# Threshold attention and a hard-swish feed-forward layer in one kernel: scores issued slot by slot at the start, projections from slot 11, products two slots sooner

## The chip, the cores and the metric

The kernel runs on one core of a Trainium2 chip. The metric is the device time of one execution in microseconds (us); lower is better. Three runs of the kernel before took 533.33, 536.99 and 535.21 us, a median of 535.21.

## The reference

Eight batches, eight heads, 576 positions, 64 dimensions per head. Attention keeps only keys whose score lies within `tau` of the row's maximum; its output goes through a feed-forward layer with 2,048 hidden units.

```python
scores = scale * np.matmul(q, k.transpose(0, 1, 3, 2))
thresh = np.max(scores, axis=-1, keepdims=True) - tau
scores = np.where(scores >= thresh, scores, -1000000000.0)
scores = scores - np.max(scores, axis=-1, keepdims=True)
attn = np.exp(scores)
attn = attn / (np.sum(attn, axis=-1, keepdims=True) + 1e-09)
x = np.matmul(attn, v)          # then (B * S, H * D)
h = x @ w_in
g = h * np.clip(h + 3.0, 0.0, 6.0) / 6.0
out = g @ w_out
```

## The kernel before

**Slots.** The work is cut into 144 slots, 18 to a batch (`NSLOT`). A slot is 128 query rows of two heads (a head pair's two halves lie in one slot; 576 keys each), or, in the two slots that hold the last 64 rows of each head, 64 rows of four heads. A Python loop (L467) walks over the slots and writes out every instruction in the order in which each engine takes it; nothing is reordered later. Each engine works through its own list in order, and waits where an operand isn't there yet.

**What a slot's attention takes.** TensorE (PE) computes the scores in fp32 (`burst`, L208) into the eight banks of the accumulator memory `ps`. VectorE (DVE) passes over each head's scores once (`sm_max`, L238): it copies them to `s` and takes the row maximum. GpSimd (POOL) makes the bias (L247), ScalarE (ACT) masks (L252) and takes the exponential with its sum (L257), DVE the reciprocal (L260), POOL normalises to bf16 `pn` (L265). The weights `pn` are then transposed into `pT` (or `pR`, for the slots of last rows): for most slots by a DMA that SyncE's queue (SP) issues (L276), for some early slots (`sl.on_chip`, L194) by PE and a copy by DVE (`pe_transpose`, L278). `pn` has four buffers, so that the normalisation of slot n+4 waits until slot n's transpose has landed.

**Products, projections, second layer.** `av_main` and `av_rest` (L293, L300) multiply transposed weights with V into one of two banks (`bank`, L178), and DVE copies the result to `xT` or `xR`. A chunk is 256 query rows of one batch. When its fourth head pair has been multiplied (`multiply`, L401), eight items for the first layer are put on a list, `todo1`. An item (`mm1`, L315) is 32 matmuls into one bank; then ACT (in odd slots) or DVE (in even ones) adds 3 and clips at 0 (`mm1_relu`), and DVE multiplies (`mm1_gate`, L346) into `g`. One item is taken in each slot from slot `N1` = 15 on. When a chunk's items are done, eight parts of the second layer go on `todo2`; odd slots take two of them (`second`, L457). DVE copies a finished tile to `osb` (L365) and SP writes it out (L378).

**The order in a slot** (loop at L467): the two DVE passes of slot n+1; reciprocal of n-1; copies left from the slot before; the projection's matmuls; products due in this slot; the projection's elementwise part; on-chip transposes of n-2; second layer; exponentials of n; masks of n+1; `jobs` (DVE's block transposes of Q and K); normalisation of n-1 on POOL, and its transpose's issue on SP; in even slots the burst for slots n+2 and n+3; then `issues` (loads on SP and POOL).

**Bursts.** Slots n and n+1 share two of the banks. In a burst the steps for both are interleaved, and the last ones, in the shared banks, are held by a no-op on POOL that itself waits for an earlier step of the burst (L213, L228). A burst starts only after DVE has passed over both slots before.

**Due slots** (L393 to L447) are written out by hand. With n0 = 18 b: products of the first chunk at n0 + 8, 10, 12, 14, of the second at n0 + 18, 20, 22, 24, of the last rows at n0 + 16. `load` (L82) loads one quad (four heads of a batch) of K in one piece or of Q in four. Weights are loaded in four pieces each by POOL's queue, w_in in slots 4, 6, 8, 10 and w_out in slots 12, 13, 14, 15; V in eight pieces per batch. After the loop, what is left of `todo1`, `todo2` and the last batch's products is worked off (L544 to L555).

Of the kernel before, what the change touches and what calls it, by code (L numbers as in the profile page):

```python
# [20 lines left out]
def kernel(  # L21
# [18 lines left out]
    N1 = 15  # L40
# [111 lines left out]
    load(0, 1, 10, T, by=nc.scalar)  # L152
    load(0, 0, 4, T)
    load(1, 1)
# [34 lines left out]
    for b in range(B):  # L189
        for g, t in ((0, 0), (0, 1), (1, 0), (1, 1), (None, 4), (0, 2), (0, 3), (1, 2), (1, 3)):  # L190
            for i in range(2):
                sl = Slot()
                sl.b, sl.g, sl.t, sl.i, sl.n = b, g, t, i, len(queue)
                sl.on_chip = sl.n in (1, 3, 5, 7, 8, 9, 11)  # L194
                queue.append(sl)
# [12 lines left out]
    def burst(n):  # L208
        steps = ((0, 0, P, 0), (1, 0, OWN, 0), (0, 0, P, 1), None,
                 (0, P, OWN, 0), (1, 0, OWN, 1), (0, P, OWN, 1), (1, OWN, P, 0), (1, OWN, P, 1))  # L210
        for step in steps:
# [6 lines left out]
            for a in range(2):  # L218
                c = 32 * (2 * i + a)
                c0 = score_col(n + i, a) + k0  # L220
                for quad, rows, q0 in (((2 * sl.b + sl.g, slice(0, P), sl.t * P),) if sl.t < 4 else
# [5 lines left out]
                    if (i, k0) == (1, OWN):  # L227
                        behind(mm, relay)  # L228

# [63 lines left out]
    def av_main(b, hp, chunk):  # L293
        if hp == chunk == 0:
            xT[b] = x_pool.tile([P, KI, 512], BF16, tag="xT", name="xT")
        pb = bank()[:, 0:256]
# [97 lines left out]
    for b in range(B):  # L394
        n0 = b * NSLOT
        for hp in range(NPAIR):
            at(products, n0 + 8 + 2 * hp, (b, hp, 0))
            at(products, n0 + 18 + 2 * hp, (b, hp, 1))
        at(products, n0 + 16, (b, None, None))
# [15 lines left out]
    for quad in range(2, 2 * B):  # L415
        b, g = divmod(quad, 2)
        n0 = (b - 1) * NSLOT
        when = (((4, 5), (7, 8))[g] if b == 1 else ((-2, -1), (6, 7))[g])
# [6 lines left out]
    at(jobs, 0, lambda: transpose_q(0, 4, 8))  # L425
    for n, job in ((0, lambda: transpose_k(1, 0)), (1, lambda: transpose_k(1, 1)), (2, lambda: transpose_q(1, 0, 8)),
                   (3, lambda: transpose_q(0, 8, T)), (5, lambda: transpose_q(1, 8, T))):
        at(jobs, n, job)
# [13 lines left out]
    for b in range(1, B):  # L442
        v_pieces(b, (16, 17, 18, 19, 20, 21, 22, 23) if b == 1 else [(b - 1) * NSLOT + n for n in range(8, 24, 2)])
    for i, n in enumerate((4, 6, 8, 10)):
        at(issues, n, lambda i=i: load_w_in(i))
    for i, n in enumerate((12, 13, 14, 15)):
# [5 lines left out]
    burst(0)  # L452
    sm_max(queue[0])
    for i in range(2):
# [11 lines left out]
    waiting = []  # L466
    for n, sl in enumerate(queue):  # L467
        now = n
        late_slot = n == len(queue) - 2
# [6 lines left out]
        waiting = []  # L476
        item = None
# [4 lines left out]
        multiply(n)  # L482
        if item:
            mm1_gate(item, h, mm1_relu(h, on_act=n % 2 == 1))
        if n > 1 and queue[n - 2].on_chip:
# [7 lines left out]
        if part == 3:  # L493
            waiting.append(lambda tile=(bb, mt): late.extend(mm2_out(*tile, on_act=False)))
# [5 lines left out]
        if n % 2 == 0 and n + 2 < len(queue):  # L500
            burst(n + 2)
        if n < 3 or n == 6:
# [6 lines left out]
    for copy in waiting:  # L509
        copy()  # L510
# [39 lines left out]
    for n in range(len(queue), len(queue) + 7):  # L550
# [39 lines left out]
```

## Time and profile before

| | |
|---|---|
| median of three runs | 535.21 us |
| profiled execution, its own time | 535.49 us |
| span, first to last instruction | 533.7 us |
| mean granted clock of PE | 0.971 of full speed |
| PE busy | 501.8 us (94%), 6,735 matmuls |
| DVE busy | 446.7 us (84%) |
| ACT busy | 442.6 us (83%) |
| POOL busy | 281.1 us (53%) |
| score matmuls (L224) | 190.4 us |
| first layer (L313, w_in) | 133.8 us |
| second layer (L313, w_out) | 130.7 us |
| products (L290) | 46.5 us |
| chain that ended last | PE 80%, DMA 4%, DVE 2% |
| DMA moved | 80.85 MB, 151 GB/s over the span |
| w_in piece, issue to landing | 8.3 us (median of 4) |
| w_out piece, issue to landing | 10.6 us (median of 4) |
| transposes pT by DMA, issue to landing | 4.0 us (median of 123) |

Busy times are unions of an engine's instructions within the span. PE runs several matmuls of a few rows at once, and their ends are modelled, so that the sums by line overlap. The chain follows the last instruction back to what released it, step by step.

### The profile page before, as it was taken

How to read it: one execution, taken by the hardware profiler on the slowest of the kernel's cores; microseconds unless marked ns; L12 is line 12 of the kernel's file. 1: busy time of each engine (PE TensorE's matmuls, PEld its weight loads, DVE VectorE, ACT ScalarE, POOL GpSimd, SP SyncE). 2: the span in 40 equal slices, each digit the busy share in tenths (PEclk: the TensorE clock that was granted, in tenths of full speed). 3: DMA queues.
4: the chain of work that ended last, by engine and by line, in shares of the span. 5: the costliest groups of instructions: out<-in, count | busy, mean ns of one | idle time of the engine just before them, and what ended most of it. 6: DMA issues, size and time to landing. Idle time of an engine off the chain costs nothing.

```text
span 533.7 us, 17090 instructions
## 1 busy us (share of the span) xinstructions
PE 501.8 (94%) x6735; PEld 371.2 (70%) x6739; DVE 446.7 (84%) x1141; ACT 442.6 (83%) x949; POOL 281.1 (53%) x512
## 2 busy tenths in 40 slices
PE   6677787999999999999999999999999999999997
PEld 6454565677777777677767777677767777778465
DVE  6664776799999999999999999999999998887433
ACT  3776676899999999999999999999999999999322
POOL 1664564655565665566665655555555556555000
PEclk9987788899999999999999999999999999999999
DMA  8499699998999969898979999997999987856511
GB/s 176 57 160 218 106 128 178 174 215 136 156 161 180 184 138 185 142 174 155 194 144 183 175 157 174 160 186 127 169 169 197 159 111 143 143 111 113 120 60 41
DMA packets 229969, 80.85 MB, mean 151 GB/s; under 512 B 210688, under 2 KB 223232, under 8 KB 229888
## 3 DMA queue, kind: packets, MB, share of 16 engines
q1 hardware_dynamic: 216016, 70.12, 77.1%
q0 software_dynamic: 13440, 8.92, 14.1%
q8 instruction: 53, 0.87, 0.7%
q10 hardware_dynamic: 432, 0.72, 0.4%
q14 instruction: 28, 0.23, 0.1%
HBM read 36.70 MB, written 9.44 MB: 86 GB/s over the span
## 4 chain that ended last, share of the span: by engine, by line
PE 80%; DMA 4%; DVE 2%; issue 1%; ACT 0%; POOLq 0%; POOL 0%; DVEq 0%
PE ps L313 46%; PE ps L224 27%; PE ps L290 6%; DMA pT<-pn 4%; DVE s L238 1%; PE ps L518 1%; ACT r L331 0%; DVE g L346 0%; DVE xT L298 0%; DVE osb L521 0%; POOLq L265 0%; POOL pn L265 0%; DVE rinv L260 0%; DVEq L260 0%; DVEq L238 0%
## 5 line engine op out<-in xcount | busy, mean ns | idle before, releaser
L238 DVE TENSOR_SCALAR_CACHE_REDUCE s<-ps 128x576 f32<-128x576 f32 x288 | 205.6, 751 | 42.5 <-PE ps L224 23.5
L252 ACT ACTIVATE s<-s,bias 128x576 f32<-128x576 f32 x288 | 205.9, 763 | 25.6 <-POOL bias L247 25.4
L265 POOL TENSOR_SCALAR pn<-s,rinv 128x576 bf16<-128x576 f32 x288 | 210.9, 745 | 23.3 <-DMA pT<-pn 4.2
L224 PE MATMUL ps<-kT,qT 32*128 32x128 f32 (+3 forms) x2560 | 190.4, 438 | 21.7 <-DVE s L238 11.7
L257 ACT ACTIVATE s<-s 128x576 f32<-128x576 f32 x288 | 192.4, 671 | 0.0
L224 PEld LDWEIGHTS ps<-kT,qT 32*128 32x128 f32 (+1 forms) x2560 | 135.4, 182 | 63.3 <-DVE s L238 16.4
L313 PE MATMUL ps<-xT,w_in_sb 128*64 128x256 bf16 (+1 forms) x1936 | 133.8, 277 | 0.1
L313 PE MATMUL ps<-w_out_sb,g 128*64 128x512 bf16 (+1 forms) x1021 | 130.7, 379 | 0.2
L313 PEld LDWEIGHTS <-w_in_sb 128*64 128x64 bf16 (+1 forms) x1936 | 110.2, 110 | 28.6 <-issue 18.3
L247 POOL TENSOR_SCALAR bias<-m 128x2 f32<-128x2 f32 (+1 forms) x146 | 27.6, 189 | 175.9 <-DVE rinv L260 165.4
L346 DVE SCALAR_TENSOR_TENSOR g<-r,ps 128x512 bf16<-128x512 f32 x128 | 87.8, 687 | 10.7 <-ACT r L331 6.3
L313 PEld LDWEIGHTS <-g 128*64 128x64 bf16 (+1 forms) x1024 | 61.7, 109 | 47.9
L331 ACT ACTIVATE r<-ps,three 128x512 f32<-128x512 f32 x81 | 55.3, 686 | 40.7 <-PE ps L313 39.7
L257 ACT ACTIVATION_READ_ACCUMULATOR s<-s 128x1 f32 x288 | 54.8, 190 | 0.0
L290 PE MATMUL ps<-pT,v 128*64 128x256 bf16 x640 | 46.5, 277 | 0.8 <-DVE s L238 0.8
L290 PEld LDWEIGHTS <-v 128*64 128x64 bf16 x960 | 42.0, 112 | 3.6 <-issue 1.5
L333 DVE TENSOR_SCALAR r<-ps 128x512 f32<-128x512 f32 x63 | 42.9, 681 | 0.0
L126 POOL DMA_DIRECT2D v<-in_v_dram x64 | 36.7, 574 | 9.4 <-issue 3.5
L298 DVE CAST xT<-ps 128x256 bf16<-128x256 f32 x64 | 26.8, 419 | 11.3 <-PE ps L290 11.1
L365 DVE TENSOR_SCALAR osb<-ps 128x512 f32<-128x512 f32 x32 | 21.5, 672 | 9.1 <-PE ps L313 9.1
L118 DVE STREAM_TRANSPOSE kT<-nk 128x320 f32<-128x320 f32 (+1 forms) x64 | 26.5, 453 | 1.0 <-DMA nk<-in_k_dram 1.0
L104 DVE STREAM_TRANSPOSE qT<-nq 128x640 f32<-128x640 f32 (+2 forms) x33 | 24.8, 751 | 0.0
(31 smaller groups left out, 143.2 us busy)
## 6 DMA issues: line engine op xcount, KB each, us to landing
nk<-in_k_dram SPq DMA_DIRECT2D x15, 576.0 KB, 5.8
nq<-in_q_dram SPq DMA_DIRECT2D x60, 144.0 KB, 5.6
out_dram<-osb SPq DMA_DIRECT2D x31, 256.0 KB, 2.9
v<-in_v_dram POOLq DMA_DIRECT2D x32, 80.0 KB, 3.9
v<-in_v_dram POOLq DMA_DIRECT2D x32, 64.0 KB, 3.5
w_in_sb<-in_moe_w_in_dram POOLq DMA_DIRECT2D x4, 512.0 KB, 8.3
w_out_sb<-in_moe_w_out_dram POOLq DMA_DIRECT2D x4, 512.0 KB, 10.6
pT<-pn SPq DMA_TRANSPOSE x123, 4.0
```

What stands on the lines that cost most here:

```text
L126: nc.gpsimd.dma_start(out=vsb[b % 2][32 * g:32 * g + 32].rearrange("p (hp a) c -> p a hp c", a=2)[:, a, :, c0 * D:(c0 + count) * D], in_=v ...
L224: mm = nc.tensor.matmul(ps_flat[rows, c0:c0 + w], qT[c:c + 32, j, q0:q0 + rows.stop - rows.start], kT[c:c + 32, j, k0:k0 + w], start=(j == ...
L238: nc.vector.tensor_scalar(out=sl.s[:, i, :], in0=ps_flat[:, c0:c0 + S], scalar1=1.0, scalar2=None, op0=Alu.mult, op1=Alu.max, accum_out=sl ...
L247: nc.gpsimd.tensor_scalar(out=sl.bias[:, of], in0=sl.m[:, of], scalar1=-scale, scalar2=tau, op0=Alu.mult, op1=Alu.add)
L252: nc.scalar.activation(out=s, in_=s, func=Act.Prelu, bias=sl.bias[:, i:i + 1], scale=scale, alpha=REJECT)
L257: nc.scalar.activation(out=s, in_=s, func=Act.Exp, accum_out=sl.rsum[:, i:i + 1])
L265: nc.gpsimd.tensor_scalar(out=pn[:, i, :], in0=sl.s[:, i, :], scalar1=sl.rinv[:, i:i + 1], scalar2=1.0, op0=Alu.mult, op1=Alu.mult)
L290: nc.tensor.matmul(pb[a * 64:(a + 1) * 64, :], vsb[b % 2][:, 2 * hp + a, u * D:(u + 1) * D], pT[:, block, cols], start=(c == 0), stop=(c = ...
L313: nc.tensor.matmul(out[c:c + w], lhsT[:, c:c + w], rhs, start=start, stop=stop)
L331: nc.scalar.activation(out=r, in_=hps, func=Act.Relu, bias=three[:])
L333: nc.vector.tensor_scalar(out=r, in0=hps, scalar1=3.0, scalar2=0.0, op0=Alu.add, op1=Alu.max)
L346: nc.vector.scalar_tensor_tensor(out=out, in0=r, scalar=6.0, in1=hps, op0=Alu.min, op1=Alu.mult)
```

## The change

Up to slot 12 the scores are no longer written out in bursts of two slots but by a new function, `scores`, one slot at a time: scores of slot n+2 are issued in slot n, at its head. What kept the shared banks apart in a burst (the no-op on POOL) is here a no-op on DVE (`pass_on`) that waits for the scores of n+1 and releases the shared part of those of n+2. Bursts return in slot 12, for slots 14 and 15.

Projections begin in slot 11 (`N1`). In every slot the products now stand ahead of the projection, and a finished second-layer tile is copied after the projection's elementwise part. All products are due two slots sooner, those of the first chunk of batch 0 in slots 6, 7, 9 and 10; in slots before `N1` they go to a bank of their own. Loads of quads 2 and 3 are due two or three slots later, V pieces of later batches two sooner, weight pieces in other slots; K of quad 1 is loaded by ACT's queue and ahead of the rest of Q. The set of slots that PE transposes changes, some early block transposes on DVE move up, and two groups of warm-up transposes on PE go.

```diff
-    N1 = 15
+    N1 = 11
...
     load(0, 1, 10, T, by=nc.scalar)
+    load(1, 1, by=nc.scalar)
     load(0, 0, 4, T)
-    load(1, 1)
     load(1, 0)
...
-                sl.on_chip = sl.n in (1, 3, 5, 7, 8, 9, 11)
+                sl.on_chip = sl.n in (1, 3, 5, 6, 7, 8)
...
+    gate = [None]
+
+    def scores(n):
+        sl = queue[n]
+        quads = [(2 * sl.b + sl.g, slice(0, P), sl.t * P)] if sl.t < 4 else [
+            (2 * sl.b + g, slice(64 * g, 64 * g + 64), 512) for g in range(2)]
+        own = (P, OWN) if n % 2 == 0 else (0, OWN)
+        shared = (0, P) if n % 2 == 0 else (OWN, P)
+        for k0, w in (own, shared):
+            for j in range(2):
+                for a in range(2):
+                    c = 32 * (2 * (n % 2) + a)
+                    c0 = score_col(n, a) + k0
+                    for quad, rows, q0 in quads:
+                        qT, kT = qkT[quad]
+                        mm = nc.tensor.matmul(ps_flat[rows, c0:c0 + w],
+                                              qT[c:c + 32, j, q0:q0 + rows.stop - rows.start],
+                                              kT[c:c + 32, j, k0:k0 + w], start=(j == 0), stop=(j == 1))
+                        if (k0, w) == shared and gate[0] is not None:
+                            behind(mm, gate[0])
+        sl.last_mm = mm
+
+    def pass_on(n):
+        gate[0] = nc.vector.nop()
+        behind(gate[0], queue[n].last_mm)
...
-        pb = bank()[:, 0:256]
+        pb = ps[:, OB, P:P + 256] if now < N1 else bank()[:, 0:256]
...
-            at(products, n0 + 8 + 2 * hp, (b, hp, 0))
-            at(products, n0 + 18 + 2 * hp, (b, hp, 1))
-        at(products, n0 + 16, (b, None, None))
+            at(products, n0 + 6 + 2 * hp if b else (6, 7, 9, 10)[hp], (b, hp, 0))
+            at(products, n0 + 16 + 2 * hp, (b, hp, 1))
+        at(products, n0 + 14, (b, None, None))
...
-        when = (((4, 5), (7, 8))[g] if b == 1 else ((-2, -1), (6, 7))[g])
+        when = (((6, 7), (9, 10))[g] if b == 1 else ((-2, -1), (6, 7))[g])
...
-    at(jobs, 0, lambda: transpose_q(0, 4, 8))
-    for n, job in ((0, lambda: transpose_k(1, 0)), (1, lambda: transpose_k(1, 1)), (2, lambda: transpose_q(1, 0, 8)),
-                   (3, lambda: transpose_q(0, 8, T)), (5, lambda: transpose_q(1, 8, T))):
+    for n, job in ((0, lambda: transpose_k(1, 0)), (0, lambda: transpose_k(1, 1)), (1, lambda: transpose_q(1, 0, 8)),
+                   (2, lambda: transpose_q(0, 8, T)), (4, lambda: transpose_q(1, 8, T))):
...
-[(b - 1) * NSLOT + n for n in range(8, 24, 2)])
-    for i, n in enumerate((4, 6, 8, 10)):
+[(b - 1) * NSLOT + n for n in range(6, 22, 2)])
+    for i, n in enumerate((4, 5, 7, 9)):
         at(issues, n, lambda i=i: load_w_in(i))
-    for i, n in enumerate((12, 13, 14, 15)):
+    for i, n in enumerate((11, 13, 15, 17)):
         at(issues, n, lambda i=i: load_w_out(i))
...
-    burst(0)
+    scores(0)
+    pass_on(0)
     sm_max(queue[0])
+    scores(1)
+    transpose_q(0, 4, 8)
...
     for n, sl in enumerate(queue):
         now = n
+        if n <= N1:
+            pass_on(n + 1)
         if n + 1 < len(queue):
             sm_max(queue[n + 1])
...
+        if n <= N1:
+            scores(n + 2)
+        multiply(n)
         item = None
         if todo1 and n >= N1:
             item, then = todo1.pop(0)
             h = mm1(item, 0 if n == len(queue) - 1 else OB if n > N1 and n % 2 == 0 and not pieces else HB)
             todo2.extend(then)
-        multiply(n)
-        if item:
             mm1_gate(item, h, mm1_relu(h, on_act=n % 2 == 1))
+        for tile in outs:
+            late.extend(mm2_out(*tile, on_act=False))
+        outs = []
...
-        if n % 2 == 0 and n + 2 < len(queue):
+        if n > N1 and n % 2 == 0 and n + 2 < len(queue):
             burst(n + 2)
-        if n < 3 or n == 6:
+        if n < 2:
             warm_up(6)
...
-    for n in range(len(queue), len(queue) + 7):
+    for n in range(len(queue), len(queue) + 5):
         multiply(n)
```

More of the change, by code (lines that the diff above doesn't have):

```diff
@@ L442 @@
     for b in range(1, B):
-        v_pieces(b, (16, 17, 18, 19, 20, 21, 22, 23) if b == 1 else [(b - 1) * NSLOT + n for n in range(8, 24, 2)])
-    for i, n in enumerate((4, 6, 8, 10)):
+        v_pieces(b, (16, 17, 18, 19, 20, 21, 22, 23) if b == 1 else [(b - 1) * NSLOT + n for n in range(6, 22, 2)])
+    for i, n in enumerate((4, 5, 7, 9)):
         at(issues, n, lambda i=i: load_w_in(i))
-    for i, n in enumerate((12, 13, 14, 15)):
+    for i, n in enumerate((11, 13, 15, 17)):
         at(issues, n, lambda i=i: load_w_out(i))
@@ L466 @@
     waiting = []
+    outs = []
     for n, sl in enumerate(queue):
         now = n
-        late_slot = n == len(queue) - 2
+        if n <= N1:
+            pass_on(n + 1)
         if n + 1 < len(queue):
@@ L481 @@
             todo2.extend(then)
-        multiply(n)
-        if item:
             mm1_gate(item, h, mm1_relu(h, on_act=n % 2 == 1))
+        for tile in outs:
+            late.extend(mm2_out(*tile, on_act=False))
+        outs = []
         if n > 1 and queue[n - 2].on_chip:
@@ L493 @@
         if part == 3:
-            waiting.append(lambda tile=(bb, mt): late.extend(mm2_out(*tile, on_act=False)))
+            outs.append((bb, mt))
             part = 0
@@ L507 @@
         prev = sl
-    for copy in waiting:
-        copy()
+    for tile in outs:
+        late.extend(mm2_out(*tile, on_act=False))
     count = [1, 0 if todo2 and todo2[0][2] else 1]
```

## The prediction

> **What bounds the kernel now.** I read the 40 slices first, then busy time by stage, the chain of waits, and the order of time around one slot.
>
> ```profile
> PE   6677787999999999999999999999999999999997
> PEclk9987788899999999999999999999999999999999
> 56.00:70.00 14.00, 12.68 (x99) 8.71 (x95) 8.51 (x25) 8.25 (x19) 7.41 (x13) 0.64 0.66 97
> 84.00:98.00 14.00, 10.18 (x100) 7.58 (x100) 8.20 (x23) 9.11 (x22) 6.51 (x12) 0.76 1.37 177
> 140.00:440.00 300.00, 299.04 (x4358) 222.71 (x4356) 285.13 (x729) 276.56 (x599) 175.59 (x319) 1.00 1.01 165
> ```
>
> The last three rows give a stretch, its length, the busy time of PE, PE's weight loads, DVE, ACT and POOL, granted clock, DMA share and GB/s. There are two regimes. From about 105 us PE is busy without a gap (299.04 of 300 us); before that it idles, and its clock is at times near half. So only the first 105 us have room, and whatever adds a wait to PE later is paid in full.
>
> I call the start of DVE's first score pass of slot n+1 the start of slot n. In order of time, slots 1, 3, 5, 7, 9, 11, 13, 15 and 17 start at 16.05, 22.73, 28.76, 36.48, 43.19, 52.93, 61.69, 69.76 and 76.07, slots 22, 26 and 142 at 95.35, 108.21 and 485.81. From 26 to 142 that is 377.6 / 58 = 6.51 us per pair of slots. Ahead of that, pairs take 6.0 to 9.7 us with far less work on PE, because a burst makes DVE and PE take turns: a burst of two slots (2.2 us, or 4.25 at 65.35 with a low clock), then two passes, then the next. From 70 to 98 us the chain goes through transfers:
>
> ```profile
> 76.89 13.75 DMA pT<-pn
> 90.91 1.28 PE ps L224 x8
> 92.47 7.17 DMA pT<-pn
> ```
>
> These are transposes held up beside the w_out loads (12.7 us from issue to landing for the load at 72.99). POOL waits for them, and a burst's last part waits for POOL.
>
> **Slots 1 to 10, scores slot by slot.** Scores of slot n+2 run while DVE passes over n+1, so each engine's own sum per slot counts. ACT: from exp at 83.60 to exp at 86.27, 2.67 us. POOL: 0.19 bias + 1.46 norm + 1.11 for two V pieces = 2.76 (0.79 for a weight piece). DVE: 1.44 for passes and reciprocal plus 0.4 to 1.9 of copies and transposes. PE: half a burst, 1.1 us, plus 0.67 and 0.7 for transposes and product; at the low clock about twice that, 2.2 to 4.5. I take 2.75 per slot. The DVE no-op added to each slot waits for the scores of n+1, and the passes behind it would wait for them anyway: 0. If PE runs cold in slots 7 to 10, it costs about 1.5 in each, 6 in all; bounds 0 and 6, I take 0, as PE's longest gap should be well under the 3 us it has before its bursts now.
>
> Slot 1: scores(0) from 6.6 take 1.1, its pass 1.4, Q transpose 0.44, pass(1) 1.4, two K transposes 1.7, waiting for K of quad 1 (lands 12.28 now; issued earlier on ACT, ahead of the rest of Q). Start 13.2 instead of 16.05. Moving that load past Q may cost Q up to 2 us; it may also gain 1. I take 0. Ten slots: slot 11 at 13.2 + 27.5 = 40.7.
>
> **Moved loads.** On SP, K of quad 2 now stands behind the transpose of slot 4 (norm near 28), so it is issued near 29; DVE wants it in slot 7, near 31.5, in the order unchanged there. Its twin took 5.0 us now, with one weight piece beside it; two will be in flight. It lands at 34 to 36, and DVE's passes queue behind the K transpose. DVE leads by about 1 us: cost 3 (0 to 6). Slot 11 at 43.7. One transpose more goes by DMA (slots 9 and 11 against 6): 4 us each, hidden behind the two or more slots until its product. The two warm-ups dropped (0.88 each) lie in PE's idle time.
>
> **Slots 11 to 22.** Projections start here, four slots sooner, and bursts return at slot 12. Slots 15 to 19 show this regime: pairs of 6.31 and 6.08, so 3.08 per slot; 11 x 3.08 = 33.9. Slot 22 at 77.6. w_out pieces come every second slot now, not every slot, which shortens the queue; but the products of slots 16 and 20 need transposes of 12 and 16, four slots back where six were. Bounds: 0 (transposes at the usual 4.0) to 16 (13.75 again, below). I take 1.5, as the pieces are spread: 79.1, against 95.35 now.
>
> **From slot 22 on: the new wait.** Products stand ahead of the projections. At b x 18 + 12 and + 22 a chunk's fourth product is followed in the same slot by the first projection that reads it; the item list is empty there, by the slots written out in both versions. Until now that projection came a slot later. One even slot, word for word:
>
> ```profile
> 108.21 0.75 DVE L238 TENSOR_SCALAR_CACHE_REDUCE s<-ps 128x576 f32<-128x576 f32 x1
> 108.40 1.04 PE L313 MATMUL ps<-xT,w_in_sb 128*64 128x256 bf16 x16
> 109.28 0.71 PE L290 MATMUL ps<-pT,v 128*64 128x256 bf16 x10
> 109.56 0.16 DVE L260 RECIPROCAL rinv<-rsum 128x2 f32<-128x2 f32 x1
> 110.23 0.41 DVE L298 CAST xT<-ps 128x256 bf16<-128x256 f32 x1
> ```
>
> With the product first, PE starts it at 108.4, is done at 109.0 (0.55 in the chain), and runs the projection's first six matmuls (three row blocks, 0.2). The seventh needs the copy. DVE is in its passes until 109.64, copies until 110.05, and PE resumes near 110.2. PE waits 1.0; burst and everything behind it on PE follow late. A pair without second-layer work takes 6.08, so DVE and ACT leave 0.4 of slack, but PE has none. Fourteen such slots (22, 30, 40, ... 138): 14.0; bounds 7 (if DVE's pass comes sooner) and 20.
>
> Late transposes: slot 24's norm ends at 109.34 and slot 28 starts at 114.83, 5.5 us later. The median landing (4.0) fits; behind a quad's loads it doesn't: slot 78's lands at 291.35, slot 82 starts at 290.05. Over the batches, counting one delay per bunch, 1.3 + 2.0 + 1.4 = 4.7; the waits above give transfers some room: I take 3 (0 to 15).
>
> The Trainium skill speaks against this half of the change: "DMA: Bandwidth & Descriptors", Rules for kernel authors, says to issue a DMA early and wait on its semaphore late, and here the wait moves two slots earlier. By that rule all of the closer products lose, and the sum would take the upper bound, 15 for 3: 541; by the rows only those behind loads do: 529.
>
> **Sum.** Start of slot 22: 79.1. Sixty pairs to slot 142 at 6.51: 390.6. Waits for the copy 14.0, late transposes 3. From slot 142 to the end now 533.7 - 485.8 = 47.9; three projections (1.04), four second-layer parts (1.89 per two) and one product (0.55) fewer are left: 47.9 - 7.4 = 40.5. Span 527.2; with 1.8 around it (535.49 - 533.7) 529.0. The profiled run lies 0.28 above the median of 535.21, so the two can be taken as one. Some 16 us are gained at the start, 17 are given back in the loop, and 7.4 less is left at the end.
>
> **Clock.** The trace has 0.64 from 56 to 70 us and 1.00 from 70 to 84; pairs there take 8.8 and 8.1 against 6.2. That is most of the room in slots 11 to 15. The skill, "TensorE: Matmul & The Clock Gate", Part 1, has the gate fall to half after an idle window of about 3.4 us; scores in every slot would then keep it open. By the rule the cold cost is 0 (529), by the rows up to 6 (535).
>
> **Rivals.** (1) Slower: transfers hold the start. If transposes of 12 and 16 take 13.75 as now, not 4.0, each product is 13.75 - 5.5 = 8.2 late, the head of PE's slot with projection and burst behind it: 16.4, less the 1.5 taken, so 544. For it: DMA share of 1.37 there, more transposes in a row. Against: pieces two slots apart, and today's stall of 6 us in slots 18 to 23 is in 95.35 already. It turns to slower (540.8) from 13 us of lateness on. (2) No change: cold PE (6) or K of quad 2 (3 more) use up part of the start: 533 to 538. Here too belongs that scores slot by slot don't do what they say, because PE's order with product and transposes ties them to DVE's copies: at 3.2 per slot instead of 2.75, 534. (3) Faster by more: the copy hardly holds PE, because DVE comes to it sooner; with 4 in place of 14, 519.
>
> **How the numbers follow.** My forecast, 529.0 with its own spread of 522 to 533, gets 0.44, of which 0.31 below 529.9; (3) 0.13; (2) 0.18; (1) 0.25. About 1% (5.35 us) is what a measurement tells from no change. Faster by over 1% (below 529.9): 0.31 + 0.13 = 0.44. Within 1%: the forecast's upper part 0.13 and (2), 0.31. Slower (above 540.6): 0.25. The range 517 to 545 takes in (3), (2) and the price of (1); beyond it lie lateness in every batch and a start without any wait.
>
> **What would show it.** In the new profile: slot 11 near 44, slot 22 near 79; idle of about 1 us on PE in front of the projections, released by DVE's xT copy, 14 times, none in other even slots; 6.5 per pair elsewhere; idle before products released by pT transposes, 3 in all after slot 24; the granted clock at 0.9 or more up to 70 us. Wrong it is if slot 22 starts after 90, if the copy's wait is under 0.5, or if transposes hold PE by 15 or more.

## The result and the profile after

The changed kernel takes 558.02 us (median of four runs, 551.52 to 559.61), beside 535.06 for the kernel before on the same chip: 1.0405 of it, 95% interval 1.0315 to 1.0495. It is slower by 4%, and 558 lies outside the predicted range of 517 to 545. The profiled execution took 558.5 us with a span of 556.7.

Slot starts are read as in the prediction. "Loop" is slot 26 to slot 142.

| | before | predicted | after |
|---|---|---|---|
| slot 0 | 10.28 | not given | 16.64 |
| slot 1 | 16.05 | 13.2 | 19.80 |
| slot 11 | 52.93 | 43.7 | 72.67 |
| slot 22 | 95.35 | 79.1 | 116.62 |
| slot 26 | 108.21 | 93.1 (79.1 + two pairs + one copy wait) | 136.94 |
| loop | 377.60 | 393.6 (377.6 + 13 copy waits + 3) | 377.38 |
| slot 142 to the end | 47.9 | 40.5 | 42.4 |

So all of the loss is made before slot 26: 28.7 us there, 0.2 and 5.5 less afterwards, 23.0 in the span. The page after, its slices for TensorE and its clock:

```profile
PE   7999996887899999999999999999999999999997
...
PEclk8555559988999999999999999999999999999999
```

A slice is 13.9 us. Slices 2 to 6 show two things at once that no slice of the kernel before showed: TensorE busy 9 tenths or more, and its clock at half. Busy time by stretch (columns as in the prediction: the stretch, its length, PE, weight loads, DVE, ACT, POOL, granted clock, DMA share, GB/s):

```profile
14.00:70.00 56.00, 56.00 (x301) 32.95 (x299) 27.22 (x78) 31.86 (x68) 24.48 (x46) 0.50 0.58 97
...
136.00:515.00 379.00, 367.68 (x5518) 271.94 (x5514) 353.42 (x915) 350.08 (x760) 219.45 (x398) 1.00 0.95 158
```

From 14 to 70 us PE has not one gap, at a clock of 0.50, with 301 matmuls; the other engines work half the time. The chain of waits says with what (start, length, what; L246 is `scores`, L309 the transposes on PE, L317 the products):

```profile
54.22 1.07 PE ps L309 x9
55.30 4.14 PE ps L246 x16
59.44 1.07 PE ps L309 x9
60.51 4.14 PE ps L246 x16
64.65 1.21 PE ps L317 x10
```

One slot's scores take 4.14 us. That is as long as a burst of two slots takes at the low clock in the kernel before (4.25 at 65.35), and nothing but PE is on the path. Later in the start the chain goes through transfers again:

```profile
108.90 9.59 DMA pT<-pn
...
126.53 2.74 DMA v<-in_v_dram
```

The first is the transpose of slot 17, for which a product waits, the second a V piece of batch 1. In the loop the expected wait is there. Groups of instructions from 136 to 515 us (busy time, mean ns, idle time before them and its releaser):

```profile
L224 PE MATMUL ps<-kT,qT 32*128 32x448 f32 (+3 forms) x2048 | 129.8, 414 | 0.6 <-DVE s L265 0.6
L340 PE MATMUL ps<-xT,w_in_sb 128*64 128x256 bf16 x1664 | 112.0, 274 | 9.1 <-DVE xT L325 9.1
```

9.1 us of idle PE in front of the projections, 13 times 0.7, released by the copy to xT. And yet the loop is not longer. If PE's matmuls from slot 26 to 142 are laid end to end without their overlaps, those of the scores cover 138.6 us before and 125.8 after, those of both layers 204.9 and 207.4, and the idle time is 1.9 before and 11.3 after: the scores look 12.8 us shorter, and the new wait and the longer projections eat that up. The wait itself costs what was foreseen: the 13 pairs of slots that hold one take 7.26 us on average, the other 45 take 6.29. Two questions follow: what made the start so slow, and what paid for the copy's wait.

### The profile page after: what moved, and what is told of

It is laid out like the page before. It is cut to its first block, busy times and chain, and to the rows that moved or that the text cites. A ratio compares the mean times of both kernels' runs of the same rounds, so it can differ in the third digit from the quotient of the medians.

```text
span 556.7 us, 17228 instructions
## 1 busy us (share of the span) xinstructions
PE 524.0 (94%) x6758; PEld 375.5 (67%) x6758; DVE 445.2 (80%) x1142; ACT 441.8 (79%) x947; POOL 280.8 (50%) x512
## 3 DMA queue, kind: packets, MB, share of 16 engines
q0 software_dynamic: 13440, 8.92, 13.2%
## 4 chain that ended last, share of the span: by engine, by line
PE 77%; DVE 13%; DMA 4%; issue 2%; ACT 2%; POOL 0%; SPq 0%; DVEq 0%; POOLq 0%
PE ps L340 36%; PE ps L224 23%; PE ps L246 10%; DVE s L265 6%; PE ps L317 6%; DMA pT<-pn 3%; DVE g L373 3%; ACT r L358 2%; DVE xT L325 1%; PE ps L309 1%; DMA nq<-in_q_dram 1%; DVE r L360 1%; DVE go L373 1%; PE ps L553 1%; DMA nk<-in_k_dram 1%
## 5 line engine op out<-in xcount | busy, mean ns | idle before, releaser
L265 DVE TENSOR_SCALAR_CACHE_REDUCE s<-ps 128x576 f32<-128x576 f32 x288 | 205.2, 749 | 35.8 <-PE ps L246 20.7
L224 PE MATMUL ps<-kT,qT 32*128 32x128 f32 (+3 forms) x2304 | 148.4, 417 | 2.8 <-DVE s L265 2.8
L340 PE MATMUL ps<-xT,w_in_sb 128*64 128x256 bf16 (+1 forms) x1960 | 139.5, 279 | 9.4 <-DVE xT L325 9.3
L224 PEld LDWEIGHTS ps<-kT,qT 32*128 32x128 f32 (+1 forms) x2304 | 110.5, 176 | 42.4 <-issue 7.7
L340 PEld LDWEIGHTS <-w_in_sb 128*64 128x64 bf16 (+1 forms) x1960 | 109.0, 111 | 21.5 <-issue 13.7
L373 DVE SCALAR_TENSOR_TENSOR g<-r,ps 128x512 bf16<-128x512 f32 x128 | 87.3, 682 | 13.9 <-ACT r L358 10.3
L317 PEld LDWEIGHTS <-v 128*64 128x64 bf16 x960 | 42.8, 114 | 29.6 <-issue 15.5
L317 PE MATMUL ps<-pT,v 128*64 128x256 bf16 x640 | 49.3, 287 | 12.2 <-DMA pT<-pn 4.5
L246 PE MATMUL ps<-kT,qT 32*128 32x448 f32 (+3 forms) x256 | 54.6, 698 | 2.6 <-DVE qT L104 2.6
L360 DVE TENSOR_SCALAR r<-ps 128x512 f32<-128x512 f32 x65 | 44.6, 687 | 14.5 <-PE ps L340 14.0
L246 PEld LDWEIGHTS ps<-kT,qT 32*128 32x128 f32 (+1 forms) x256 | 29.7, 296 | 26.8 <-issue 20.0
L126 POOL DMA_DIRECT2D v<-in_v_dram x64 | 36.7, 574 | 19.0 <-PE ps L224 14.9
L325 DVE CAST xT<-ps 128x256 bf16<-128x256 f32 x64 | 26.0, 406 | 22.8 <-PE ps L317 22.7
L392 DVE TENSOR_SCALAR osb<-ps 128x512 f32<-128x512 f32 x32 | 21.8, 683 | 7.0 <-PE ps L340 7.0
```

The lines of the kernel that those rows point to most:

```text
L126: nc.gpsimd.dma_start(out=vsb[b % 2][32 * g:32 * g + 32].rearrange("p (hp a) c -> p a hp c", a=2)[:, a, :, c0 * D:(c0 + count) * D], in_=v ...
L224: mm = nc.tensor.matmul(ps_flat[rows, c0:c0 + w], qT[c:c + 32, j, q0:q0 + rows.stop - rows.start], kT[c:c + 32, j, k0:k0 + w], start=(j == ...
L246: mm = nc.tensor.matmul(ps_flat[rows, c0:c0 + w], qT[c:c + 32, j, q0:q0 + rows.stop - rows.start], kT[c:c + 32, j, k0:k0 + w], start=(j == ...
L265: nc.vector.tensor_scalar(out=sl.s[:, i, :], in0=ps_flat[:, c0:c0 + S], scalar1=1.0, scalar2=None, op0=Alu.mult, op1=Alu.max, accum_out=sl ...
L317: nc.tensor.matmul(pb[a * 64:(a + 1) * 64, :], vsb[b % 2][:, 2 * hp + a, u * D:(u + 1) * D], pT[:, block, cols], start=(c == 0), stop=(c = ...
L340: nc.tensor.matmul(out[c:c + w], lhsT[:, c:c + w], rhs, start=start, stop=stop)
```

## Experiments

Sixteen kernels ran. Kernels run together share one chip and one set of runs of before (533.68, 533.29, 535.83 and 533.62 us in the four sets: e1 to e4, e5 to e8, e9 to e12, e13 to e16). Nine kernels ran once (e2, e3, e4, e7 to e11, e15); the four runs of the change itself lie 8 us apart, so their slot starts and stretches say more than small differences of their times. The kernels stand here by question. In e1 to e4, theory A is that scores written slot by slot, which fill only half of the array, make the loss; the other letters put it elsewhere.

### The scores: bursts, slots, and the clock

**e1_bursts**: the change, with bursts from the start as before.

```diff
-    scores(0)
-    pass_on(0)
+    burst(0)
...
-            pass_on(n + 1)
...
-            scores(n + 2)
...
-        if n > N1 and n % 2 == 0 and n + 2 < len(queue):
+        if n % 2 == 0 and n + 2 < len(queue):
```

> The changed kernel with bursts of two slots from the first slot on; everything else of the change stays (projections from 11, products sooner and ahead, loads). Theory A: the loss is in the scores issued slot by slot, because the matmuls of one slot fill two of the four groups of 32 rows that a burst fills, so a slot costs as much as a burst of two, and PE so half-filled never gets its full clock. Then slot 11 starts at 50 to 55 us, not 72.7, no stretch of 70 us at half clock, and the time is 527 to 538. Rival B (the moved loads, on-chip set and closer products cost it): slot 11 still after 65, time 550 or more.

It took 551.32 us (1.035 of before, 1.0282 to 1.0419). The time at half clock up to slot 26 shrank from 81.9 us to 47.8, slot 11 came at 66.8 in place of 72.7, slot 26 at 130.0, still 21.8 after before's. Time and slot 11 are the rival's: the slot-wise scores are not the only cause.

**e2_scores**: the other way round, the kernel before with `scores` and `pass_on` up to slot 12, the earlier block transposes and the products' own bank that these need, and nothing else of the change.

```diff
+    NS = 11
...
+        if n <= NS:
+            pass_on(n + 1)
...
+        if n <= NS:
+            scores(n + 2)
...
-        if n % 2 == 0 and n + 2 < len(queue):
+        if n > NS and n % 2 == 0 and n + 2 < len(queue):
```

> The kernel before with scores slot by slot up to slot 12, and nothing else of the change but the block transposes that this order needs: projections from 15, products, loads and on-chip set as before. Theory A: slot 11 starts at 66 to 75 us, clock half from about 10 to 80 us, time 550 to 562. Rival B: within 1% of the kernel before, 530 to 540.

It took 549.44 us, just under the range of theory A; slot 11 came at 67.7 (52.9 before) and slot 26 at 122.2 (14.0 late), and the clock was at half without a break from 13.3 to 78.2. The loop took 377.6, as before. On its own this part costs 14 us.

**e3_warm**: the change, with 12 transposes of 128x128 on PE added in each of slots 0 to 10, into columns that nothing reads.

```diff
...
-        if n < 2:
-            warm_up(6)
+        if n < N1:
+            warm_up(12)
```

> The changed kernel with twelve full-array warm-up transposes at the end of each of slots 0 to 10, in columns that nobody reads (two slots had six). If the low filling of the array holds the clock (A), the extra work lets it rise: the mean score matmul of the early slots falls from 698 to 350 to 500 ns, slot 11 starts at 52 to 64, time 538 to 550, although PE does more. Rival C (the matmuls are long because they wait for DVE's no-ops): the mean stays near 700 ns, slots get 1.6 to 3 us longer, slot 11 at 90 or later, time 570 or more.

It took 550.62 us, 0.6 over the expected range and less than any run of the change (551.52 to 559.61), although PE does more. Up to 80 us only 13.7 are at half clock, from 8.9 to 22.5. Its chain (L162 is the added work):

```profile
33.55 2.15 PE ps L246 x16
35.70 1.46 PE ps L162 x12
37.16 2.15 PE ps L246 x16
39.30 0.61 PE ps L309 x9
```

At full clock a slot's scores take 2.15 us; the mean score matmul takes 469 ns in place of 698, so waits for DVE's no-ops (rival C) don't make it long. Slot 11 came at 63.2, at the late end of what was expected, since the added transposes themselves lie on the path (34.5% of the chain from 20 to 64 us). The two numbers split the missed term: 1.1 was taken for a slot; 2.15 is what it takes on an array at full clock, and 4.14 at half clock. The first factor of two lies in the code: a slot's heads sit in rows `c = 32 * (2 * (n % 2) + a)`, two of four groups of 32 rows. A burst keeps all four groups busy (two slots in 2.2 us), one slot only two of them.

The Trainium skill has this on its page "TensorE: Matmul & The Clock Gate", section "Why this matters for your kernels": the gain of matmuls of 32 rows is that four of them run side by side (3.07 times measured there), while one alone takes as long as a full one. Here two slots on four groups took 2.2 us and one slot on two groups 2.15, which agrees.

**e4_serial**: the kernel before, a burst's steps ordered slot after slot, so that only two groups of rows work at a time.

```diff
-        steps = ((0, 0, P, 0), (1, 0, OWN, 0), (0, 0, P, 1), None,
-                 (0, P, OWN, 0), (1, 0, OWN, 1), (0, P, OWN, 1), (1, OWN, P, 0), (1, OWN, P, 1))
+        steps = ((0, 0, P, 0), (0, 0, P, 1), None, (0, P, OWN, 0), (0, P, OWN, 1),
+                 (1, 0, OWN, 0), (1, 0, OWN, 1), (1, OWN, P, 0), (1, OWN, P, 1))
```

> The kernel before with the steps of each burst put slot after slot (all of n, then all of n+1) in place of interleaved; same matmuls, same relay. This measures the row groups alone, at the full clock and without DVE no-ops. Theory A: a burst takes 4.0 to 4.3 us instead of 2.2 from slot 25 on, a pair 8.2 to 8.6 instead of 6.5, time 640 to 690. Rival C: order within a burst is free, time 532 to 542.

It took 566.82 us, far less than the 640 to 690 of theory A. A burst now takes 2.83 to 3.03 us in place of 2.36 to 2.55, not twice as long, and the loop 405.4, 0.48 more per pair. The two slots still overlap: in the burst that starts at 203.95 us the 448-column matmuls of both run four at a time (204.50 to 206.34), and only the 128-column ones at either end run in twos. A slot that stands alone has no such neighbour. The direction of theory A is confirmed, its size for this kernel was wrong.

### The start without the scores: loads and products

**e7_loads**: e1, with the loads (but for V of later batches) and the block transposes that follow the first of them in before's places; products, projections and the set transposed on PE as in the change.

```diff
-    load(1, 1, by=nc.scalar)
     load(0, 0, 4, T)
+    load(1, 1)
...
-        when = (((6, 7), (9, 10))[g] if b == 1 else ((-2, -1), (6, 7))[g])
+        when = (((4, 5), (7, 8))[g] if b == 1 else ((-2, -1), (6, 7))[g])
...
-    for i, n in enumerate((4, 5, 7, 9)):
+    for i, n in enumerate((4, 6, 8, 10)):
...
-    for i, n in enumerate((11, 13, 15, 17)):
+    for i, n in enumerate((12, 13, 14, 15)):
```

> The change with bursts (experiment e1) and with all loads, and the transposes on VectorE that follow the first of them, in before's places; products, projections and the set of slots transposed on chip as in the change. e1 took 551.3, 16 over before, with slot 11 at 66.8 (52.9 before), slot 26 at 130.0 (108.2). Theory loads (the moved loads hold the start): slot 0 back at 10 to 11, slot 11 at 53 to 58, kernel 530 to 540. Theory closer (the products and on-chip transposes of slots 6 to 10 hold it): slot 0 back at 10 to 11, but slot 11 at 60 to 63, slot 26 at 122 to 128, kernel 543 to 550.

It took 544.25 us. Slot 0 is back at 10.32, but slot 11 comes at 61.2 and slot 26 at 122.3: the theory "closer" in every number. Its chain (L265 is DVE's pass, L310 its copy of on-chip transposes):

```profile
51.06 0.67 DVE pT L310
51.73 0.04 issue
51.77 0.75 PE ps L317 x10
...
53.65 1.34 DVE s L265 x4
54.98 0.08 DVE rinv L287
55.06 0.67 DVE pT L310
55.73 0.04 issue
55.77 1.28 PE ps L317 x10
57.05 1.07 PE ps L309 x9
58.12 2.07 PE ps L224 x13
```

Nothing overlaps here. DVE passes over the scores, then copies the transposed weights; only then can the product due in that very slot start; behind it on PE stand the next transposes and the burst, and for that burst DVE waits. Products in slots 6, 7, 9 and 10, as close as that to slots transposed on PE, turn two engines into one line; from 30 to 80 us PE stood idle 8.3 us in front of products for the copy of pT.

**e8_late**: e1, with products, projections (from slot 15), the set transposed on PE and later V pieces as before; loads as in the change.

```diff
-    N1 = 11
+    N1 = 15
...
-                sl.on_chip = sl.n in (1, 3, 5, 6, 7, 8)
+                sl.on_chip = sl.n in (1, 3, 5, 7, 8, 9, 11)
...
-            at(products, n0 + 6 + 2 * hp if b else (6, 7, 9, 10)[hp], (b, hp, 0))
-            at(products, n0 + 16 + 2 * hp, (b, hp, 1))
+            at(products, n0 + 8 + 2 * hp, (b, hp, 0))
+            at(products, n0 + 18 + 2 * hp, (b, hp, 1))
```

> The other half of e7: the change with bursts, its loads as in the change, but products, projections (from slot 15), the set transposed on chip and the loads of V for later batches as before; the products ahead of the projection stay, with their copy. Theory loads: slot 0 at 14 to 17, slot 11 at 62 to 67, kernel 545 to 551. Theory closer: slot 0 at 14 to 17, slot 11 at 57 to 60, slot 26 at 112 to 117, kernel 536 to 544.

It took 539.91 us, with slot 0 at 14.92, slot 11 at 59.9, slot 26 at 114.9. With the change's loads slot 26 is 6.7 late, of which 4.6 are there at slot 0: K of quad 1 on ACT's queue, ahead of the rest of Q, delays Q (the last two of the four parts of its first piece land at 7.72 and 8.72 in the change, 5.66 and 5.98 before).

At slot 26, then: scores 14.0 (e2), products with their slots on PE 14.0 (e7), loads 6.7 (e8). The last two make 20.7, and e1, which has both, is 21.8 late. All three make 34.7 against 28.7 in the change, so some hide behind one another; how much is uncertain, as slot 26 comes anywhere from 134.0 to 139.8 in kernels that are alike up to slot 10. e7 and e8 also keep the change's order in a slot (by itself, in e5, it brings slot 26 forward by 1.6) and, like the change, do without two groups of warm-up transposes, which no run tries by itself.

**e6_closer**: the kernel before, all products two slots closer (batch 0's first in slots 6, 8, 10 and 12, where the change has 6, 7, 9 and 10), projections from 13, V pieces of later batches two slots sooner; order, other loads and the set transposed on PE as before.

```diff
-    N1 = 15
+    N1 = 13
...
-            at(products, n0 + 8 + 2 * hp, (b, hp, 0))
-            at(products, n0 + 18 + 2 * hp, (b, hp, 1))
-        at(products, n0 + 16, (b, None, None))
+            at(products, n0 + 6 + 2 * hp, (b, hp, 0))
+            at(products, n0 + 16 + 2 * hp, (b, hp, 1))
+        at(products, n0 + 14, (b, None, None))
```

> The kernel before, with all products two slots closer to the making of their weights and projections from slot 13 on, products behind the projection as before; loads, transposes on chip and scores untouched. Theory order of e5: score matmuls from 26 to 142 cover 137 to 140 us, as before, and there is no copy to wait for, so 376 to 379 us. Rival closeness: 125 to 128 us of bursts. The end: four fewer us of tail (47.9 to 43 or 44), so 528 to 533 if the start is no later, since the tail has two slots' products less; if products that wait for their transposes hold the start (slots 12 to 25), slot 26 comes after 112 us (108.2 before) and the kernel takes 534 to 542.

It took 534.39 us (1.001 of before, 0.9977 to 1.0043), with slot 26 at 111.2, the loop 377.7, the tail 43.9 in place of 47.9. Neither end of the expectation was far off: 3 lost, 4 won. In the loop the distance of two slots is of no account either way.

### The loop: what paid for the copy's wait

**e5_order**: the kernel before, a slot's product ahead of its projection, the projection still chosen first.

```diff
             item, then = todo1.pop(0)
+        multiply(n)
+        if item:
             h = mm1(item, 0 if n == len(queue) - 1 else OB if n > N1 and n % 2 == 0 and not pieces else HB)
             todo2.extend(then)
-        multiply(n)
-        if item:
```

> The kernel before, with one edit: a slot's product is issued ahead of its projection, but which projection is made is still chosen ahead of the product, so that it never needs the copy of that same product. From slot 26 to slot 142 the trace of the change shows TensorE idle 11.5 us (2.1 before), nearly all of it that copy, and the score matmuls covering 125.8 us (138.6 before): the order seems to shorten the bursts by as much as the copy's wait costs. Theory order (the shorter bursts come from the order alone): 26 to 142 takes 364 to 369 us in place of 377.6, and the kernel 520 to 527. Rival pace (the pair is paced by something else, VectorE or ScalarE, and the bursts' time was slack): 376 to 378, kernel 532 to 536. Rival closeness (bursts are shorter because the weights are two slots closer): bursts cover 137 to 139 us as before, 376 to 378.

It took 530.18 us (0.9946 of before, 0.992 to 0.9972), the loop 374.1, and the scores cover 135.1. That is none of the three theories: the order is worth 3.5 us in the loop, not 9 to 13. Read with the change, this looked as if bursts held a slack that swallows an idle PE. The next kernel was to show that.

**e9_nocopy**: the change, the projection chosen ahead of the product and issued behind it, so that none reads a copy of its own slot.

```diff
-        multiply(n)
         item = None
         if todo1 and n >= N1:
             item, then = todo1.pop(0)
+        multiply(n)
+        if item:
             h = mm1(item, 0 if n == len(queue) - 1 else OB if n > N1 and n % 2 == 0 and not pieces else HB)
```

> The change with one edit: a slot's projection is chosen ahead of its product and issued behind it, so that no projection reads a copy of its own slot; this takes the copy's wait (9.4 us of TensorE's idle time from slot 26 to 142) away and nothing else. Theory slack (found with e5: the bursts hold waits of their own for VectorE, which swallow an idle TensorE): 26 to 142 falls from 377.4 to about 374, score matmuls cover 134 to 136 us in place of 125.8, kernel 553 to 557. Theory of the prediction (each copy wait is paid in full): 366 to 369, score matmuls at 126, kernel 546 to 550.

It took 551.79 us, over the expected 546 to 550, as slot 26 came at 139.8 in place of 136.9. The loop took 366.4, and the scores cover 126.7. From 136 to 500 us:

```profile
L340 PE MATMUL ps<-xT,w_in_sb 128*64 128x256 bf16 x1648 | 108.6, 274 | 0.0
```

The slack theory falls. The copy's wait is paid: the loop is 11.0 us shorter without it, and pairs with and without the chunk's first projection now both take 6.3 us. Some of the 11.0 only moves, as 16 second-layer matmuls more are left for after slot 142; to the end 9.5 are won. Something else in the change saves as much, and it isn't the order alone.

**e10_pe** and **e11_dve**: the change, with more work on one engine in the loop; the output stays the same. In e10 each projection makes the first matmul of its two sums twice; in e11 each reciprocal is made twice.

```diff
+                if 26 <= now < len(queue) - 1:
+                    half_columns(ps[:, hb, n * 256:(n + 1) * 256], w_in_sb[:, 0, (ni + n) * P:(ni + n + 1) * P],
+                                 xT[b][:, 0, c0:c0 + 256], start=True, stop=True)
```

```diff
+        if sl.n >= 26:
+            nc.vector.reciprocal(out=sl.rinv[:], in_=sl.rsum[:])
```

> The change with more work on TensorE alone: from slot 26 on, each projection of the main tiles makes the first matmul of its two sums once more ahead of them (the sum then starts afresh, so the output is the same): 2 x 0.11 us per slot by the 0.87 us of its 16 pairs of matmuls, about 22 us from slot 26 to 142. If TensorE sets the pace of the pairs: 397 to 400 us in place of 377.4. If it has slack because VectorE or ScalarE set it: 378 to 385. If the two take turns in a ring: 388 to 396.

> The change with more work on VectorE alone: from slot 26 on, each slot's reciprocal is made twice, 0.16 us more per slot, 18.6 us from slot 26 to 142. If VectorE sets the pace: 395 to 397 us in place of 377.4. If TensorE sets it: 377 to 380, with less idle time of TensorE for the copy's sake unchanged. If the two take turns in a ring: 385 to 394.

The kernels took 575.93 and 572.62 us, the loop 397.5 and 389.3. Of 22.7 us more on PE (what both layers cover, 230.1 against 207.4) 20.2 came through; of 18.6 us more on DVE, 11.9. PE sets the pace, as the first expectation had it, but DVE is so close behind that most of its added work shows too.

So it matters where DVE's copies stand. The change moves one of them, that of a finished second-layer tile to osb, behind the projection's elementwise part. In order of time, before, one burst of slot 58 behind a finished tile:

```profile
213.28 0.67 DVE L365 TENSOR_SCALAR osb<-ps 128x512 f32<-128x512 f32 x1
...
213.55 2.55 PE L224 MATMUL ps<-kT,qT 32*128 32x128 f32 x32
...
213.86 0.41 DVE L298 CAST xT<-ps 128x256 bf16<-128x256 f32 x1
...
214.33 0.31 PEld L224 LDWEIGHTS ps<-kT,qT 32*128 32x128 f32 x8 [0.26 <-DVE xT L298]
```

In the midst of the burst a weight load waits 0.26 us for the copy to xT: the product has used a bank that the burst fills. That copy stands behind the osb copy of 0.67. The 28 bursts of the loop that stand behind a finished tile take 2.55 us (median), the others 2.36. The wait doesn't show as idle PE, since the burst's other matmuls are under way.

**e15_osb_early**: the change, with this copy back in before's place.

```diff
         waiting = []
+        for tile in outs:
+            late.extend(mm2_out(*tile, on_act=False))
+        outs = []
...
-        for tile in outs:
-            late.extend(mm2_out(*tile, on_act=False))
-        outs = []
         if n > 1 and queue[n - 2].on_chip:
```

> The change with the osb copy back at before's place on VectorE, ahead of the copy to xT. Theory osb (it is what repaid the copy's waits): 26 to 142 takes 383 to 390 us in place of 377.4, as predicted for the loop (377.6 plus waits), score matmuls cover 132 to 138 us; kernel 562 to 572. Rival (the osb copy is of no account): 376 to 379, kernel 556 to 560.

It took 568.27 us, the loop 386.7, and the scores cover 132.0. Taking back this one move costs 9.3 us in the loop.

**e13_osb**: the same move alone, on the kernel before.

```diff
             mm1_gate(item, h, mm1_relu(h, on_act=n % 2 == 1))
+        for tile in outs:
+            late.extend(mm2_out(*tile, on_act=False))
+        outs = []
...
-            waiting.append(lambda tile=(bb, mt): late.extend(mm2_out(*tile, on_act=False)))
+            outs.append((bb, mt))
```

> The kernel before, with one part of the change: the copy of a finished second-layer tile to osb comes behind the projection's elementwise part on VectorE, and no longer ahead of the product's copy to xT. Theory osb (a burst's weights for the bank that the product used wait for the xT copy, and that copy for the osb copy of 0.67 us; bursts behind a finished tile take 2.55 us, the others 2.36): both kinds take 2.36 or less, 26 to 142 takes 368 to 373 us in place of 377.6, kernel 523 to 530. Rival (the wait returns elsewhere on VectorE, which has the same work): 376 to 378, kernel 532 to 536.

That is a miss of both expectations: it took 538.71 us (1.0097 of before, 1.0058 to 1.0135), the loop 382.1, 4.5 longer. The bursts are shorter (they cover 134.8), but first and second layer cover 209.2 instead of 204.9, and PE idles 5.6 us instead of 1.9. Its chain, with the product still behind the projection:

```profile
212.12 0.42 DVE xT L298
212.55 0.61 DVE r L333
...
213.18 0.69 DVE g L346
213.87 0.60 DVE osb L365
```

The copy to xT now starts when the product ends, late in the slot, and everything else on DVE, osb last, is queued behind it; second-layer matmuls then wait for osb (1.5 us from 136 to 500) and projections for `g` (1.5). Each of the two moves needs the other: with the product first, DVE finds its result ready after the passes; with osb last, nothing stands ahead of it. Order alone 3.5 won, osb alone 4.5 lost, both 11.7 won (e14).

### Under both kernels

**e12_spread**: e5, with w_out loads in slots 11, 13, 15, 17.

```diff
-    for i, n in enumerate((12, 13, 14, 15)):
+    for i, n in enumerate((11, 13, 15, 17)):
```

> Experiment e5 (before, with products ahead of projections that do not need them; 0.9946 of before) with one part of the change added: the four w_out loads in slots 11, 13, 15 and 17 in place of 12, 13, 14 and 15. In e5 the chain holds 16.65 us of transposes from 78.9 us on, and those of slots 12 to 15 take 8.8 to 12 us from issue to landing, beside those loads; in e1, with the loads spread, 5.7 to 8.6. Theory transfers (the burst of weight loads holds the transposes): slot 26 at 102 to 106 in place of 106.6, kernel 526 to 530. Rival: the transposes wait for one another or for the loads of V, and spreading moves the stall to slots 20 to 25: slot 26 at 106 to 108, kernel 530 to 532.

It took 530.65 us (0.9902 of before, 0.9866 to 0.9938), with slot 26 at 106.2 beside e5's 106.6. The transposes of slots 13 to 15 are shorter, 6.9 to 7.4 us in place of 10.9 to 12.0, but those of 16 (10.2) and 17 (7.9) are not: the stall moved. Both numbers lie just inside the rival's ranges, but 0.4 us is too little to tell the two theories apart.

**e14_best**: e12 with the osb copy of e13.

> Experiment e12 with the later osb copy added: before's places for products, bursts and projections, products ahead of a projection chosen earlier, w_out loads spread, osb behind the projection. Theory osb: bursts 2.2 us in all pairs, 26 to 142 takes 364 to 368 us in place of 374.2, kernel 519 to 524, under both kernels. Rival (e9's 366.4 comes from weights two slots closer, or from another part of the change): 372 to 375, kernel 528 to 532.

It took 521.97 us, 0.9798 of before (0.9768 to 0.9828). The loop takes 365.9, the scores cover 126.3, and PE idles 2.1. The same burst as above, in order of time:

```profile
208.63 0.40 DVE L298 CAST xT<-ps 128x256 bf16<-128x256 f32 x1
...
208.91 2.04 PEld L224 LDWEIGHTS ps<-kT,qT 32*128 32x128 f32 x32 [0.20 <-DVE rinv L260]
208.91 2.23 PE L224 MATMUL ps<-kT,qT 32*128 32x128 f32 x32
...
210.35 0.68 DVE L365 TENSOR_SCALAR osb<-ps 128x512 f32<-128x512 f32 x1
```

The copy to xT begins before the burst does, all 32 weight loads follow one another, and the burst takes 2.23 us.

**e16_closer2**: e14 with e6's closer products and projections.

> Experiment e14 with e6 on top: all products two slots closer and projections from slot 13 on, V pieces of later batches two slots sooner. In e6 slot 26 came 3.0 us later and the tail was 4.0 us shorter, net 1 us less. Theory additive: slot 26 at 107 to 111, tail 43 to 45, kernel 517 to 523. Rival (the closer weights wait for transposes where TensorE no longer waits for the burst): 26 to 142 takes 369 us or more, kernel 524 to 530.

It took 531.19 us (0.9967 of before, 0.9941 to 0.9993), and neither expectation fits. The loop is the same, 365.8; slot 26 comes at 121.7, not at 107 to 111. One row of its chain:

```profile
86.06 11.24 DMA pT<-pn
```

A product two slots closer waits there for the transpose of slot 16 (11.2 us from issue to landing, beside the weight loads). The clock is also at half for 47.8 us up to slot 26, in place of 20.5 in e14. So the loop doesn't mind closer products, the start does, and by how much differs from kernel to kernel: 3.0 in e6, 15.6 here over e14.

## Why the prediction was wrong

The span came out 29.5 us over the predicted 527.2. By its own steps:

| step | predicted | measured | error |
|---|---|---|---|
| slot 1 starts | 13.2 | 19.80 | +6.6 |
| slots 1 to 11, with K of quad 2 | 30.5 | 52.87 | +22.4 |
| slots 11 to 22 | 35.4 | 43.95 | +8.6 |
| slots 22 to 26 | 14.0 | 20.32 | +6.3 |
| loop | 393.6 | 377.38 | -16.2 |
| from slot 142 on | 40.5 | 42.4 | +1.9 |

- **"PE: half a burst, 1.1 us"** is the step that failed. Half the work of a burst isn't half its time, because the two slots of a burst run side by side in different rows of the array: a slot's scores take 2.15 us at full clock (e3). PE's sum per slot with transposes and product was then 3.4 at full clock (2.15 + 0.61 + 0.67 in e3), not 2.5, and PE, not ACT or POOL, sets the slot. By itself this would be some 7 us in ten slots (an estimate: 3.4 for 2.75, taken for every slot, all else as predicted), which brings 529 to 536, no change; the sign came with the next step.
- **"If PE runs cold ... I take 0"** failed with it. Bounds were 0 and 6 for slots 7 to 10; all of slots 0 to 11 ran at half clock, where a slot's scores took 4.14. The reason given, that PE has no long gap, was true and did not help: there was no gap at all from 14 to 70 us. The skill's rule that was weighed there ("TensorE: Matmul & The Clock Gate", Part 1) has the clock fall after an idle window, which this kernel then did not have. The same part has some 3.4 us of sustained activity release the gate, and that is not borne out by 56.00 busy us of 56.00 at 0.50.
- **"Moving that load past Q may cost Q up to 2 us; I take 0"**: the last part of Q's first piece landed 2.7 us later (8.72 for 5.98), so the upper bound was too low. Slot 0 came 6.4 us later (in e8 4.6): slot 0's scores, at half clock, took 4.1 us to DVE's first pass in place of 2.3 for the burst, and slot 1's made it wait another 1.8. The slot-wise start of slot 1 gained 2.6 of it back (19.80 - 16.64 = 3.2 us behind slot 0, 5.8 before).
- **K of quad 2 on SP behind the transpose of slot 4**: 3 us were taken. In e1 it was issued at 36.26, landed 9.6 us later, and DVE waited 4.3 us for it, so the mechanism was right. In the change, where PE alone was on the path until 77 us, it hid behind the scores.
- **Products in slots 6 to 10** were costed as PE time only, 0.7 each. Their wait for DVE's copy in the same slot wasn't. With bursts (e7) it shows, and what e7 keeps of the change is worth 14.0 at slot 26. In the change itself PE has no gap up to 70 us, so there this wait hides behind the scores.
- **Slots 11 to 26, late transposes**: 1.5 us were taken with bounds 0 and 16; 14.9 more were lost over the two rows of the table. The chain from 95 to 137 us has 9.6 us of a transpose and 2.7 of a V piece, and the clock was at half until 81 us, so the first rival's mechanism is a part of it, short of its 16.4. Its premise was misread too: the 13.75 us were slot 15's transpose, while those of 12 and 16 took 9.8 and 8.9 before, and 7.2 and 6.1 in the change. And pairs of 6.31 and 6.08 make 3.10 per slot, not 3.08, which is 0.2 us in eleven slots.
- **The wait for the copy**: right in place, count and price. The trace has 13 waits from slot 26 on (one of the 14 lies before), 0.7 of idle PE each, and a pair with one takes 1.0 more than the others (7.26 and 6.29), as predicted. e9 shows 11.0 us for 13.0 predicted in the loop, 9.5 to the end.
- **"6.5 per pair elsewhere"** failed: it is 6.3 (6.29 in the change; 366.4 / 58 in e9). The copy to osb stands in the diff and in no step of the sum. With the product ahead of the projection it is worth what the copy's wait costs; e15 has 9.3 for it alone. So the loop as a whole came to net 0: the term that was counted was paid, and the one that was left out repaid it. That it came out as before is luck, not a sum.
- **Late transposes in the loop**: 3 predicted, 1.3 in the trace (136 to 515 us). The skill's rule to wait late ("DMA: Bandwidth & Descriptors", Rules for kernel authors), weighed at 15 us, did not bite there; e6 and e16 agree (377.7 and 365.8, as without closer products). In the start it held (e16).
- **Tail**: 7.4 predicted, 5.5 measured.

Of the rivals, none had the cause. The second named scores that don't do what they say, but put the blame on DVE's copies and 3.2 us on the slot, where 5.3 were measured.

Not settled: how much of the start's 28.7 us is clock and how much is the half-filled array, since e3 buys its clock with work on the path. A kernel in which slot-wise scores fill all four groups was not tried.

## What to carry to other kernels

Half the work is half the time only if the halves don't run side by side: before a batch of small matmuls is taken apart, look at which rows of the array each half fills. A copy on an engine that is off the chain can still sit in the midst of a burst, through a shared bank; such a wait shows as a longer group of matmuls and not as idle time, so compare the same group's length in slots with and without it. Cost every hunk of a diff, the one-line moves too: the one left out here was worth as much as the one costed with most care.

## What the runs showed of the hardware

- TensorE can be busy without a gap and keep half its clock: it had half for 71.7 us in one stretch (9.7 to 81.4), with no gap from 14 to 70, and 74% of the chain there are fp32 matmuls in two of four row groups. Twelve full-size transposes per slot, 1.46 us in some 4, lifted it after 22.5 us and kept it up until 84 (e3). That the share of the array in use counts fits both; it was not measured by itself.
- A load put ahead on one queue delayed another queue's. With K of quad 1 ahead, the first slot started at 16.64, 17.84, 14.02, 17.56 and 14.02 us in five kernels that are alike up to slot 10 (the change, e9, e10, e11, e15); with before's loads and bursts at 10.23 to 10.85 in all. The last part of Q's first piece landed at 7.07 to 9.64 us in the five, at 5.93 to 6.20 with before's loads; the rest of the delay is scores at a clock that fell early.
- DMA transposes beside weight loads took 7 to 14 us from issue to landing at the start, against a median of 4.0 overall; spreading the loads shortened those beside them and left the next ones late (e12).
